# A causal convolution in 64x32 tiles, placed behind the second product slot

## The chip, the core and the metric

One core of a Trainium2 chip. The metric is the device time of one execution in microseconds (us); lower is better. Engines by the profile's names: PE (TensorE), PEld (its weight loads), DVE (VectorE), ACT (ScalarE), POOL (GpSimd), SP (SyncE, which issues most transfers).

## The reference

`x` is 8 x 4160 x 192 in float32. First a causal convolution along the sequence, 7 taps, one softmax-normalised set of taps for each of 8 heads of 24 channels; then, per token, a maximum of three linear maps and an output map:

```python
w = softmax(weight, axis=-1)                       # 8 heads x 7 taps
y[b, s, h, g] = sum_k w[h, k] * x_pad[b, s + k, h, g]   # x_pad: 6 zero rows ahead of the sequence
h = maximum(maximum(y @ w1, y @ w2), y @ w3)       # 192 -> 768
out = h @ w_out                                    # 768 -> 192, 33280 tokens, float32
```

## The kernel before

The 33,280 tokens are 65 blocks of 512. A block is 512 consecutive tokens of one sequence, or (one block) the last 64 tokens of all eight sequences. Every block goes through three steps:

- **conv**: `y`, turned so that channels lie on partitions, in float16, twice (each row half of the 128 partitions has all 192 channels in three 64-row pieces).
- **l1** (`L490`): six column tiles `j` of the hidden layer. w3 is subtracted from w1 and w2 beforehand (`wd`: upper rows w2 - w3, lower rows w1 - w3), so that a tile takes 3 matmuls on each half of the array's rows, 64 x 128, 512 columns. The lower half gives `lp`, the upper `lq`; ACT writes r = relu(lp) (`L503`), DVE writes h = max(r, lq) (`L504`).
- **st2** (`L508`): the output, 4 groups of 128 tokens, 30 matmuls of 192 columns on each half (`po`): `h` against `w_out`, and `y` against m = w3 w_out, which brings back what was subtracted. ACT copies one half's sum (`L560`), DVE adds the other (`L561`), SP stores.

The loop over block t (`L656`) is a software pipeline: l1 of block t and st2 of block t - 1 alternate, one column tile and 5 matmuls on each half at a time. I call such a pair a product slot; there are six in an iteration.

Conv is made in three ways. Blocks 0 to 3 by dense band matmuls (`conv_dense`, `L405`). The blocks of `qpos` (11, 16, ... 61 and 64; twelve) on POOL: load, cast, transpose by SP, then 7 taps (`tap_q`, `L221`: three products `L229` and a sum `L237` a tap), spread over the iterations by `plan`. All others on PE, block 4 alone and then in pairs: POOL casts the two x blocks to float16 (`cast_x`, `L165`), `conv` (`L387`) multiplies them by a band matrix, ACT and DVE copy the four results `G` out of PSUM to `ys` (`evac`), SP turns `ys` by a DMA transpose to `yd` (`turn`) and copies each half of `yd` across to the other (`double`).

In `conv` of before a tile has 64 tokens on 70 rows (64 and the 6 ahead), 16 matmuls with 192 columns, two places of 64 columns abreast:

```python
lhsT=band[0:HALF + PAD, h, PAD:HALF + PAD],
rhs=x16s[t0][0:HALF + PAD, h, c, :, :, :].rearrange("p u r c -> p (u r c)"),
start=True, stop=True, tile_position=(0, HALF * c))
```

It stands behind l1's first tile of the iteration, with one matmul of st2's lower half drawn ahead of it (`st2(t - 1, 0, NJ, True)`). The conv of a pair is made three iterations before its first block is used.

PSUM has 8 banks: `psp` and `psq`, two each, for lp and lq in turn; `psw`, four, for po. Conv takes two of psw and one each of psp and psq. Engines run their own instructions in the program's order; SP's order in an iteration is: load x of block t + 6, double block t + 2, a lane's transpose and lead-in rows, a lane's load, (after conv) turn block t + 3, store block t - 2.

Of the kernel before, what the change touches and what calls it, by code (L numbers as in the profile page):

```python
# [14 lines left out]
P = 128  # L15
# [12 lines left out]
def kernel(  # L28
# [42 lines left out]
    qpos = [q for q in range(11, NB - 3, EVERY)] + [NB - 1]  # L71
# [23 lines left out]
    NR = NBLK // HALF  # L95

    def rows_of(t):
        rows = [(b, S + o) for (b, S, N, off) in blocks[t] for o in range(0, N, HALF)]
        assert len(rows) == NR
        return rows  # L100
# [4 lines left out]
    xfp = ctx.enter_context(tc.tile_pool(name="xfp", bufs=6))  # L105
# [5 lines left out]
    ydp = ctx.enter_context(tc.tile_pool(name="ydp", bufs=6))  # L111
# [9 lines left out]
    xin = {}  # L121

    def load_x(t, eng=nc.sync):
        if not 0 <= t < NB or t in qset:
            return
        pool, tag = (xfp, "xf") if t > 1 else ((xap, "xa"), (xbp, "xb"))[t]
        xf = pool.tile([P, NR, D], FP32, tag=tag, name=f"xf_{t}")
        if t < NDENSE:
            todo = [(0, c[3], c[1] * SEQ + c[2]) for c in chunks_of[t]]
        else:  # L130
            todo = [(PAD, HALF, b * SEQ) if s == 0 else (0, HALF + PAD, b * SEQ + s - PAD)
                    for b, s in rows_of(t)]
        parts = []
        i, n = 0, len(todo)
        row = [c[2] for c in todo]
        while i < n:
            k = i
            while k + 1 < n and todo[k + 1][:2] == todo[i][:2] and row[k + 1] - row[k] == row[i + 1] - row[i]:
                k += 1
            step = row[i + 1] - row[i] if k > i else 0  # L140
            p0, rlen = todo[i][:2]
            src = bass.AP(tensor=x.tensor, offset=row[i] * D,
                          ap=[[D, rlen], [step * D, k - i + 1], [1, D]])
            eng.dma_start(out=xf[p0:p0 + rlen, i:k + 1, :], in_=src)
            if parts and parts[-1][0] == rlen:
                parts[-1] = (rlen, parts[-1][1], k + 1)
            else:
                parts.append((rlen, i, k + 1))
            i = k + 1
        xin[t] = [xf, todo[0][0], parts]  # L150
# [14 lines left out]
    def cast_x(t):  # L165
# [4 lines left out]
        if u == 0:  # L170
            x16s[t0] = x16p.tile([P, NHEAD, 2, nu, NR // 2, GRP], FP16, tag="x16", name=f"x16_{t0}")
        if p0:
            nc.gpsimd.memset(xf[0:p0, 0, :], 0.0)
        K = HALF + PAD
        for c in range(2):
            nc.gpsimd.tensor_copy(out=x16s[t0][0:K, :, c, u, :, :].rearrange("p h r c -> p r h c"),  # L176
                                  in_=xf[0:K, c:NR:2, :].rearrange("p r (h c) -> p r h c", c=GRP))


# [41 lines left out]
    def tap_q(q, k):  # L221
# [17 lines left out]
        yd = dense[q] = ydp.tile([P, 2, NCH // 2, P], FP16, tag="yd", name=f"yd_{q}")  # L239
# [41 lines left out]
    for t in range(2, 7):  # L281
        load_x(t)

# [3 lines left out]
    nc.gpsimd.tensor_copy(out=ident16[:], in_=ident[:])  # L287
    idle = const.tile([P, NBLK], FP16)
# [25 lines left out]
    for v in range(2):  # L314
        nc.gpsimd.memset(xz[1][v][:], 0.0)
    wcol16 = const.tile([P, 3, KW], FP16)
# [70 lines left out]
    def conv(t, pools):  # L387
# [4 lines left out]
        per = NHEAD // n  # L392
        w = nu * (NR // 2) * GRP
        G = [pool.tile([P, per, w], FP32, tag=tag, name=f"G{i}_{t}") for i, (pool, tag) in enumerate(pools)]
        for h in range(NHEAD):
            for c in range(2):
                nc.tensor.matmul(  # L397
                    G[h // per][HALF * c:HALF * (c + 1), h % per, :],
                    lhsT=band[0:HALF + PAD, h, PAD:HALF + PAD],
                    rhs=x16s[t0][0:HALF + PAD, h, c, :, :, :].rearrange("p u r c -> p (u r c)"),  # L400
                    start=True, stop=True, tile_position=(0, HALF * c))
        slots[t0] = ysp.tile([P, nu, NR // 2, D], FP16, tag="ys", name=f"ys_{t}")
# [35 lines left out]
    def evac(t, i, copy=nc.scalar.copy):  # L438
# [3 lines left out]
        per = NHEAD // len(G)  # L442
        copy(out=slots[t][:, :, :, GRP * per * i:GRP * per * (i + 1)].rearrange(  # L443
# [3 lines left out]
    def turn(t):  # L447


        if t >= NB or t in qset:  # L450
            return
        t0, u, nu = place(t)
        yd = dense[t] = ydp.tile([P, 2, NCH // 2, P], FP16, tag="yd", name=f"yd_{t}")
        nc.sync.dma_start_transpose(out=yd[:, 0, :, :],
                                    in_=slots[t0][:, u, :, :].rearrange("p r d -> p (r d)"))

    def double(t):

        if NDENSE <= t < NB:
            yd = dense[t]  # L460
            for i in range(2):
                nc.sync.dma_start(out=yd[HALF * i:HALF * (i + 1), 1, :, :],
                                  in_=yd[HALF * (1 - i):HALF * (2 - i), 0, :, :])

    def spot(t, i, c, r):
# [3 lines left out]
        else:  # L469
            own, k = (NC * r + c) % 2, (NC * r + c) // 2  # L470
        return k + (0 if own == i else NCH // 2)

    def y_all(t, i, c):
        row = slice(HALF * i, HALF * (i + 1))
        if t < NDENSE:
            return dense[t][row, c, :]
        a = dense[t][row, 0, 0, :]
# [5 lines left out]
    def y_tok(t, i, c, s):  # L483
        row = slice(HALF * i, HALF * (i + 1))
        if t < NDENSE:
            return dense[t][row, c, P * s:P * (s + 1)]
        k = spot(t, i, c, s)
        return dense[t][row, k // 6, k % 6, :]

    def l1(t, j, pools=((psp, "p"), (psq, "q"))):  # L490


        N = blkN[t]
        ps = [pool.tile([P, NBLK], FP32, tag=tag, name=f"l{tag}{i}_{t}_{j}")
              for i, (pool, tag) in enumerate(pools)]
        for c in range(NC):
            for i in range(2):
                row = slice(HALF * i, HALF * (i + 1))
                nc.tensor.matmul(ps[i][:, 0:N], lhsT=wd[row, c, P * j:P * (j + 1)],  # L499
                                 rhs=y_all(t, i, c),  # L500
                                 start=(c == 0), stop=(c == NC - 1))
        r = rp.tile([P, NBLK], FP16, tag="r", name=f"r_{t}_{j}")
        nc.scalar.activation(out=r[:, 0:N], in_=ps[0][:, 0:N], func=AF.Relu)  # L503
        nc.vector.tensor_max(out=hs[t][:, j, 0:N], in0=r[:, 0:N], in1=ps[1][:, 0:N])  # L504

    ahead = set()

    def st2(t, u, NU, first_half_only=False):  # L508
# [5 lines left out]
        hT = hs[t]  # L514
        if t not in halves:
            todo = [[], []]
            for s in range(4):
                for i in range(2):
                    row = slice(HALF * i, HALF * (i + 1))
                    mm = [(y_tok(t, i, i, s), m16[row, 0, :])]  # L520
                    if s % 2 == i:
                        mm.append((y_tok(t, i, 2, s), m16[row, 1, :]))
                    hh = [(hT[row, j, P * s:P * (s + 1)], wo[row, j, :]) for j in range(NJ)]
                    mm = hh + mm if t == 0 else mm + hh
                    todo[i] += [(s, n == 0, n == len(mm) - 1, m) for n, m in enumerate(mm)]
# [6 lines left out]
            halves[t] = (todo, {})  # L532
        todo, ps = halves[t]
        n = len(todo[0])
        es = range(n * u // NU, n * (u + 1) // NU)
        for e in es[:1] if first_half_only else es:
            for i in range(2):
                if first_half_only:
                    if i:
                        break  # L540
                    ahead.add((t, e))
                elif i == 0 and (t, e) in ahead:
                    continue
                s, first, last, (a, b) = todo[i][e]
                b0 = s if t == NB - 1 else s - s % 2
                if (b0, i) not in ps:
                    pool, tag = (psw, "w")
                    if t == NB - 1 and s in (1, 2):
                        pool, tag = (psp, "p") if i == 0 else (psq, "q")
                    ps[b0, i] = pool.tile([P, 2, D], FP32, tag=tag, name=f"po{i}_{t}_{s}")  # L550
                nc.tensor.matmul(ps[b0, i][:, s % 2, :], lhsT=a, rhs=b, start=first, stop=last)  # L551
            ends = {todo[i][e][0] for i in range(2) if todo[i][e][2]}
            for s in sorted(ends):
                done[t, s] = done.get((t, s), 0) + sum(todo[i][e][0] == s and todo[i][e][2] for i in range(2))
                if done[t, s] < 2 or (s % 2 == 0 and t < NB - 1):
                    continue
                s0 = s if t == NB - 1 else s - 1
                ss = slice(s0 % 2, s % 2 + 1)
                a = tp.tile([P, 2, D], FP32, tag="a", name=f"a_{t}_{s}")
                nc.scalar.copy(out=a[:, ss, :], in_=ps[s0, 0][:, ss, :])  # L560
                nc.vector.tensor_add(out=outs[t][:, s0:s + 1, :], in0=a[:, ss, :],  # L561
                                     in1=ps[s0, 1][:, ss, :])
                if t == NB - 1 and s == 1:
                    store(t, 0, 2, (nc.sync,))
                elif t == NB - 1 and s == 3:
                    store(t, 2, 3, (nc.scalar,))
                    store(t, 3, 4, (nc.sync,))
# [17 lines left out]
    def begin(t):  # L585
        hs[t] = hp.tile([P, NJ, NBLK], FP16, tag="h", name=f"h_{t}")
# [168 lines left out]
```

## Time and profile before

| | |
|---|---|
| median of 3 runs | 464.19 us (463.25 to 464.36) |
| the profiled execution | 464.5 us, span 462.7 us, clock granted 1.0 throughout |
| PE po, line 551 | 3120 + 780 matmuls of 192 columns, 243 ns each |
| PE lp and lq, line 499 | 2 x 1158 matmuls recorded, 512 columns, 376 ns each |
| PE G, line 397 | 400 matmuls, 248 ns each; 400 weight loads |
| POOL taps, lines 229, 237, 240 | 252 x 478 ns, 60 x 1809 ns, 12 x 1814 ns |
| POOL casts, line 176 | 98 x 822 ns |
| copies of G, line 443 | ACT 49 x 484 ns, DVE 49 x 550 ns |
| transfers | 80.77 MB, mean 175 GB/s; queue 1 busy 79.1% of 16 engines' span |

The matmul durations overlap: a matmul's row runs from its start to its end at the far side, while the next one on the same rows starts earlier. Distances between starts say what a matmul occupies. The span begins with the first instruction and ends with the last; some 1.8 us of the execution lie around it.

### The profile page before, as it was taken

To read this page: it belongs to the slowest core of one execution; us is meant where nothing else is said; L and a number is where in the kernel's file an instruction comes from. 1 tells how busy PE (TensorE), PEld (TensorE's weight loads), DVE (VectorE), ACT (ScalarE), POOL (GpSimd) and SP (SyncE) were. 2 spreads that over 40 slices of the span, in tenths; PEclk is the share of its full clock that TensorE was granted. 3 is DMA by queue.
4 is the path that set the end of the run, shared out by engine and by line. 5 is a ranking of instruction groups with operands and counts; after the bars stand their busy time and mean duration, and the time that the engine had idled before them with its cause. 6 is when DMAs were issued, how large, how long until landed. Compare 5 with 4: busy or idle time off the path is not lost.

```text
span 462.7 us, 17259 instructions
## 1 busy us (share of the span) xinstructions
PE 454.4 (98%) x6969; PEld 367.9 (80%) x6969; DVE 354.1 (77%) x595; ACT 314.3 (68%) x597; POOL 352.6 (76%) x501
## 2 busy tenths in 40 slices
PE   8999999999999999999999999999999999999997
PEld 4576788977877887888888888888888888888886
DVE  6777777777778787777878777777777777777775
ACT  5766566667676666767667676676767676676664
POOL 5753289999988978978967978978957969979500
PEclk9999999999999999999999999999999999999999
DMA  8959999999869878787789697698598797884423
GB/s 190 222 127 198 177 209 179 192 209 224 192 130 231 170 155 211 175 181 183 166 175 198 157 211 165 157 213 198 132 210 179 164 224 176 144 191 92 100 70 103
DMA packets 137527, 80.77 MB, mean 175 GB/s; under 512 B 58294, under 2 KB 137368, under 8 KB 137448
## 3 DMA queue, kind: packets, MB, share of 16 engines
q1 hardware_dynamic: 137176, 79.18, 79.1%
q8 instruction: 54, 0.88, 0.9%
q0 software_dynamic: 112, 0.39, 0.3%
q14 instruction: 25, 0.20, 0.2%
q10 hardware_dynamic: 160, 0.10, 0.1%
HBM read 29.85 MB, written 25.56 MB: 120 GB/s over the span
## 4 chain that ended last, share of the span: by engine, by line
PE 89%; POOL 5%; DMA 4%; issue 1%; DVE 0%; ACT 0%; POOLq 0%; DVEq 0%; SPq 0%
PE lq L499 35%; PE po L551 33%; PE lp L499 14%; PE G L397 4%; POOL tap L237 2%; POOL tap L229 2%; DMA yd<-ys 1%; PE idle L294 1%; DMA xt<-xq 1%; DMA yd<-yd 1%; PE D L415 1%; POOL x L176 1%; DMA xt<-xt 1%; PE lw L499 0%; PE band_cols L335 0%
## 5 line engine op out<-in xcount | busy, mean ns | idle before, releaser
L504 DVE TENSOR_TENSOR h<-r,lq 128x512 f16<-128x512 f16 x386 | 264.7, 686 | 99.5 <-ACT r L503 99.4
L503 ACT ACTIVATE r<-lp 128x512 f16<-128x512 f32 x386 | 230.5, 597 | 134.7 <-PE lp L499 123.8
L499 PE MATMUL lp<-yd,wd 64*128 64x512 f16 x1158 | 312.3, 376 | 2.2 <-DMA yd<-yd 1.6
L499 PE MATMUL lq<-yd,wd 64*128 64x512 f16 x1158 | 312.3, 376 | 0.3 <-DVE yd L431 0.3
L551 PE MATMUL po<-wo,h 64*128 64x192 f16 x3120 | 263.8, 243 | 0.7 <-issue 0.7
L551 PEld LDWEIGHTS <-h 64*128 64x128 f16 x3120 | 209.2, 94 | 22.2 <-issue 0.9
L499 PEld LDWEIGHTS <-wd 64*128 64x128 f16 x2340 | 160.9, 94 | 39.4 <-DMA yd<-yd 2.1
L176 POOL CAST x<-xf 70x768 f16<-70x768 f32 x98 | 77.8, 822 | 60.6 <-DMA xf<-in_x_dram 54.0
L229 POOL TENSOR_SCALAR tap<-xt,wcol 128x256 f32<-128x256 f16 x252 | 116.1, 478 | 3.9 <-DMA xt<-xt 3.3
L237 POOL TENSOR_TENSOR tap<-tap,tap 128x768 f32<-128x768 f32 x60 | 108.6, 1809 | 5.0
L551 PE MATMUL po<-m,yd 64*128 64x192 f16 x780 | 109.4, 243 | 0.0
L561 DVE TENSOR_TENSOR o<-a,po 128x384 f32<-128x384 f32 (+1 forms) x132 | 71.4, 541 | 1.2 <-ACT a L560 1.2
L551 PEld LDWEIGHTS <-yd 64*128 64x128 f16 x780 | 61.9, 94 | 11.8
L560 ACT COPY a<-po 128x384 f32<-128x384 f32 (+1 forms) x132 | 62.3, 473 | 3.0 <-PE po L551 3.0
L443 DVE CAST ys<-G 128x384 f16<-128x384 f32 x49 | 24.9, 550 | 0.6 <-PE G L397 0.6
L397 PEld LDWEIGHTS <-band 70*64 70x64 f16 x400 | 15.8, 109 | 9.9 <-PE lp L499 9.0
L240 POOL TENSOR_TENSOR yd<-tap,tap 128x768 f16<-128x768 f32 x12 | 21.8, 1814 | 1.0
L397 PE MATMUL G<-x,band 70*64 70x192 f16 (+1 forms) x400 | 21.2, 248 | 0.7 <-POOL x L176 0.5
L443 ACT CAST ys<-G 128x384 f16<-128x384 f32 x49 | 21.0, 484 | 0.8 <-PE G L397 0.8
L198 POOL CAST xq<-xl 128x384 f16<-128x384 f32 x24 | 11.4, 505 | 0.0
L256 POOL CAST xz<-xf 112x80 f16<-112x80 f32 (+2 forms) x18 | 5.2, 330 | 4.5 <-DMA xf<-in_x_dram 4.5
L294 PE MATMUL idle<-idle 128*128 128x512 f16 x15 | 6.4, 573 | 1.2 <-DVE idle L289 1.2
(52 smaller groups left out, 68.6 us busy)
## 6 DMA issues: line engine op xcount, KB each, us to landing
out_dram<-o SPq DMA_DIRECT2D x61, 384.0 KB
xf<-in_x_dram SPq DMA_DIRECT2D x47, 420.0 KB
yd<-yd SPq DMA_DIRECT2D x122, 96.0 KB
xl<-in_x_dram SPq DMA_DIRECT2D x12, 384.0 KB
xf<-in_x_dram SPq DMA_DIRECT2D x5, 367.5 KB
ws<-in_moe_w_dram SPq DMA_DIRECT2D x6, 192.0 KB
out_dram<-o SPq DMA_DIRECT2D x5, 192.0 KB
yd<-ys SPq DMA_TRANSPOSE x49
```

Of the source, the lines that this page charges most:

```text
L176: nc.gpsimd.tensor_copy(out=x16s[t0][0:K, :, c, u, :, :].rearrange("p h r c -> p r h c"), in_=xf[0:K, c:NR:2, :].rearrange("p r (h c) -> p ...
L229: nc.gpsimd.tensor_scalar(out=part[:, 2 * c:2 * c + 2, :], in0=xt[:, 2 * c:2 * c + 2, LEAD - PAD + k:LEAD - PAD + k + P], scalar1=wcol[:, ...
L237: nc.gpsimd.tensor_add(out=accs[q][:], in0=accs[q][:], in1=part[:])
L240: nc.gpsimd.tensor_add(out=yd[:, 0, :, :], in0=accs.pop(q)[:], in1=part[:])
L397: nc.tensor.matmul(G[h // per][HALF * c:HALF * (c + 1), h % per, :], lhsT=band[0:HALF + PAD, h, PAD:HALF + PAD], rhs=x16s[t0][0:HALF + PAD ...
L443: copy(out=slots[t][:, :, :, GRP * per * i:GRP * per * (i + 1)].rearrange("p u r (h c) -> p h (u r) c", c=GRP), in_=G[i][:].rearrange("p h ...
L499: nc.tensor.matmul(ps[i][:, 0:N], lhsT=wd[row, c, P * j:P * (j + 1)], rhs=y_all(t, i, c), start=(c == 0), stop=(c == NC - 1))
L503: nc.scalar.activation(out=r[:, 0:N], in_=ps[0][:, 0:N], func=AF.Relu)
L504: nc.vector.tensor_max(out=hs[t][:, j, 0:N], in0=r[:, 0:N], in1=ps[1][:, 0:N])
L551: nc.tensor.matmul(ps[b0, i][:, s % 2, :], lhsT=a, rhs=b, start=first, stop=last)
L560: nc.scalar.copy(out=a[:, ss, :], in_=ps[s0, 0][:, ss, :])
L561: nc.vector.tensor_add(out=outs[t][:, s0:s + 1, :], in0=a[:, ss, :], in1=ps[s0, 1][:, ss, :])
```

## The change

- **Conv's tiles**: 32 tokens on 39 rows (32 and 7 ahead), in both row halves and in four column places, so eight places; 64 matmuls for a pair, 96 columns each. An x block is loaded as 16 pieces of 39 rows, 8 below and 8 above, in two DMAs instead of one; the rows between are zeroed once by POOL (six buffers, now constant tiles). A cast covers 103 partitions; its free size stays 768.
- **Its place**: behind l1's second column tile of the iteration. Ahead of it stand 7 of st2's lower matmuls and 3 of its upper ones (`OWN`, `AHEAD`), the upper half's four follow after it. The slots behind it are filled by `ROOM`: st2 is at 5, 13, 17, 21, 26, 30 matmuls at the end of the slots instead of 5, 10, 15, 20, 25, 30.
- **The order of matmuls**: the halves have queues of their own (`lanes`); `emit` writes out the one with fewer columns so far, `meet` empties both ahead of conv. Before, they alternated strictly. What ACT, DVE and SP do after certain matmuls (`op`) is written out when these have been.
- **Turn and double**: both transposes of a pair directly behind conv; one doubling of both blocks (two DMAs of 192 KB instead of four of 96) two iterations ahead of the first of them, on SP now in front of the x load.
- **Ten GpSimd blocks** (15, 20, ... 60) instead of twelve: 25 pairs on PE instead of 24. The first taps are in iteration 8 instead of 5, over five iterations.
- **The store of block 0** moves from POOL to SP; stores of block t - 2 are still in iteration t, now ahead of turn.

The core of the diff:

```diff
-    qpos = [q for q in range(11, NB - 3, EVERY)] + [NB - 1]
+    qpos = [q for q in range(15, NB - 4, EVERY)]
...
+    TOK = 32
+    NR = NBLK // TOK // 2
+    LAP = PAD + 1
+    KR = TOK + LAP
...
         for h in range(NHEAD):
-            for c in range(2):
-                nc.tensor.matmul(
-                    G[h // per][HALF * c:HALF * (c + 1), h % per, :],
...
+            for j in range(4):
+                for i in range(2):
+                    row = slice(HALF * i, HALF * i + KR)
+                    nc.tensor.matmul(
+                        G[2 * (h // per) + i][TOK * j:TOK * (j + 1), h % per, :],
+                        lhsT=band[row, h, HALF * i + LAP:HALF * i + KR],
+                        rhs=x16s[t0][row, h, j, :, :, :].rearrange("p u r c -> p (u r c)"),
+                        start=True, stop=True, tile_position=(HALF * i, TOK * j))
...
+    def emit(rest=False):
+        run_ops()
+        while lanes[0] or lanes[1]:
+            i = 0 if clock[0] <= clock[1] else 1
+            if not lanes[i]:
+                if not rest:
+                    return
+                i = 1 - i
+            cols, fn = lanes[i].popleft()
+            fn()
+            clock[i] += cols
+            gone[i] += 1
+            run_ops()
+
+    def meet():
+        emit(True)
+        assert not ops
+        clock[0] = clock[1] = 0
...
+        st2(t - 1, (cuts[0], cuts[0]))
         for j in range(1, NJ):
             l1(t, j)
-            st2(t - 1, j, NJ)
+            if late and j == 1:
+                st2(t - 1, (cuts[0] + OWN + AHEAD, cuts[0] + OWN))
+                meet()
+                conv(u, WPWQ)
+                for i in (0, 2):
+                    evac(u, i)
+                for i in (1, 3):
+                    evac(u, i, nc.vector.tensor_copy)
+                turn(u)
+            st2(t - 1, (cuts[j], cuts[j]))
```

## The prediction

> **What bounds the kernel now.** I read the page's busy shares first, then the chain that ended last, then single stretches of TensorE (PE) in the timeline, then the waits.
>
> ```profile
> PE 454.4 (98%) x6969; PEld 367.9 (80%) x6969; DVE 354.1 (77%) x595; ACT 314.3 (68%) x597; POOL 352.6 (76%) x501
> PE 89%; POOL 5%; DMA 4%; issue 1%; DVE 0%; ACT 0%; POOLq 0%; DVEq 0%; SPq 0%
> ```
>
> PE is the bound. But a busy PE is not a full one: the question is what it streams in each stretch. The chain, in order of time, gives the beat (two convolutions, shown with what follows them):
>
> ```profile
> 114.57 0.85 PE G L397 x16
> 115.42 0.52 PE po L551 x9
> 116.59 0.40 PE po L551 x8
> 117.65 0.40 PE po L551 x8
> ...
> 128.25 0.85 PE G L397 x16
> ```
>
> One product slot (an `l1` of 3+3 matmuls of 512 columns, then 5+5 of 192 columns, lower and upper row half abreast) takes 1.06 us (116.59 to 117.65), six slots a block, 6.36. The convs of pairs start at 114.57, 128.25 and, 5 blocks after the first, at 148.33: 33.76 us for 30 slots (31.80) and two convs. So one pair's conv costs (33.76 - 31.80) / 2 = 0.98 us of PE. Where that goes is seen in the timeline of PE:
>
> ```profile
> 114.07 0.38 PE L499 MATMUL lp<-yd,wd 64*128 64x512 f16 x1
> 114.27 0.38 PE L499 MATMUL lq<-yd,wd 64*128 64x512 f16 x1
> 114.28 0.24 PE L551 MATMUL po<-m,yd 64*128 64x192 f16 x1
> 114.57 0.27 PE L397 MATMUL G<-x,band 70*64 70x192 f16 x2
> ...
> 115.35 0.26 PE L551 MATMUL po<-m,yd 64*128 64x192 f16 x2
> ```
>
> A 512-column matmul holds its half 0.216 us (lp to lp in these rows), a 192-column one 0.082. The lower half is free at 114.36, the upper (it runs 0.2 late) at 114.48; G begins at 114.57, 0.09 after the later half; its 16 matmuls stream until 115.25; the products begin again 0.10 later. So 0.98 = 0.11 lower half idle + 0.09 + 0.68 + 0.10.
>
> **The conv, part by part.** Before: 24 pairs and one single block, 16 matmuls each, two abreast. After: 25 pairs and a single, 64 matmuls of 96 columns on 39 rows and 32 columns, eight places. Rows that bound one such conv:
>
> ```profile
> 28.33:28.80 0.47, 0.47 (x40) 0.47 (x42) 1.00 0.00 0
> 29.35:29.70 0.35, 0.34 (x16) 0.35 (x16) 1.00 0.00 0
> ```
>
> These are two stretches of PE, the first of the dense conv (line 415, four 32-column places abreast, 103 columns), the second of the single block's conv (line 397, two abreast, 96 columns). The second says that a 96-column round takes 0.35 / 8 = 0.043 us; the first that four places abreast still keep this rate (10 rounds in 0.47, 0.047 for 103 columns). That two row halves run abreast, every slot shows. Eight abreast no row shows. Lower bound: 64 / 8 = 8 rounds, 0.34 us. Upper bound: PE takes in no more than the first row's 40 matmuls and 42 loads in 0.47, so 64 pairs in 0.74; 16 rounds, if the halves do not overlap here, give 0.69. I take 0.37, near the lower end, because the first row scaled with the columns and not with the count.
>
> The Trainium skill (TensorE: Matmul & The Clock Gate, Part 3, "Measured speedup vs the span model") puts a further place at some 4 ns; by that 64 would need an estimated 0.26 us and streaming would bind; by the dense row's rate it would be 0.74 and nearly all of the gain gone. No run here shows eight places.
>
> Around it: the 0.09 and 0.10 stay (the tile form still changes twice). The 0.11 goes if both halves end together: the lower half takes 7 second products, the upper 3, and the upper's four go after the conv, so each half has the same work from conv to conv. But conv results must leave PSUM before the next slots. With the rows' durations (relu 0.597, max 0.686, ys copies 0.484 on ACT and 0.550 on DVE), from the moment E when the halves end: DVE finishes the max of slot 1 at E+0.95, its two copies at E+1.4 and E+1.9; slot 2's upper product wants that max at E+0.96, slot 3's products want the two buffers at E+1.6 and E+2.0; the second pair of po tiles wants ACT's two copies (E+1.0, E+1.5) at E+1.45 and E+1.8. All fit within 0.05. So one conv: 0.09 + 0.37 + 0.10 + 0.04 = 0.60 (bounds 0.55 and 0.93, or 0.25 more if DVE comes late).
>
> Sum: 25 x 0.60 = 15.0 instead of 24 x 0.98 = 23.5: **-8.5 us**. The single block's conv, 0.35 now, lies between 0.17 (8 rounds of 48 columns) and 0.74; it is put at no change, since the transfer after it ends later anyway.
>
> **GpSimd.** Two conv blocks fewer take 2 x (21 x 0.478 + 5 x 1.809 + 1.814 + 2 x 0.505 + 0.19) = 44 us off POOL; four more casts (0.822, free size unchanged) and six zero fills (1,536 columns; from the 960 of line 315 in 0.892, 1.4 each) add 12. POOL is off the path but for one place:
>
> ```profile
> 80.08 0.24 PE L397 MATMUL G<-x,band 70*64 70x192 f16 x1
> 80.84 0.82 PE L397 MATMUL G<-x,band 70*64 70x192 f16 x15 [0.53 <-POOL x L176]
> ```
>
> Here the first lane's taps, packed into three iterations, keep the cast late; with what precedes it PE loses 1.0. The first lane now starts its taps at iteration 8 instead of 5 and spreads them over five: **-1.0**. The fills lie in the start, where POOL waits 4.5 us for loads.
>
> **SyncE and transfers.** A pair's two transposes now go together, a slot and a half later, and the next iteration's doubling waits for them, with the x loads behind it on SP (before, the load went first). Issue to landing, by the semaphores: transposes 2.8, doubles 4.7, x loads 6.1 us (medians after 100 us). From an iteration's start: copies done 4.1, second transpose landed 4.1 + 1.25 + 2.8 = 8.2, that is 1.2 into the next (6.96 long); doubles issued by 2.4, landed about 7.5, wanted at 13: covered by 5 us. Loads issued by 3.0, landed 9.1, cast 1.6, wanted by the conv in the iteration after at 15.3 on the same count: spare 4.4. Cover gone, each us late costs each conv a us. The stores moved to SP are issues of 0.5 us of outputs finished an iteration ago: nothing behind them waits. In the start PE waits twice for doubles:
>
> ```profile
> PE lp L499 <- DMA yd<-yd: 1.6, 2, 0.9
> ```
>
> With the drain before them they are 1.1 us (block 4) and 0.9 (block 5). Block 4 gets a second transpose (1.3 us of issue) in its way; block 5's doubling loses the load and store that stood in front of it. They may vanish (-1.9) or grow by 1: put at 0. At the end the upper half trails by two 192-column matmuls more: +0.15.
>
> An x block grows from 8 x 70 to 16 x 39 rows, 420 to 468 KB. A five-block beat moves 33.76 us x 182 GB/s (200 to 300 us) = 6.14 MB now and 6.34 in 33.0 us after, 192 GB/s; 40 to 80 us already moved 198, and the share there was 1.01 against 0.82. So it fits, with less air.
>
> The Trainium skill speaks against this edit (DMA: Bandwidth & Descriptors, "Why a DMA increments its semaphore by 16 and not by 1"): the engines used are the largest number up to 16 that divides the outer row counts, 14 for 70 rows, 13 for 39. By it the x share would sit on 13 engines, 36 KB of a block on each instead of 30, and my estimate of a beat on those (1.92 MB / 13 + 4.42 MB / 16, at 198 GB/s / 16) is 34 us instead of 33.0: no gain left, some 464. The shares of this trace are means over 16 engines and cannot show it.
>
> **Sum.** -8.5 - 1.0 + 0 + 0.15 = -9.3. Span 462.7 becomes 453.4; the profiled execution took 464.5, 1.8 around its span: 455.2; the median of the runs, 464.19, lies 0.3 lower: **455.0 us**.
>
> **Rivals.** (a) PE's intake, or halves that do not overlap: conv 0.69 to 0.74, 25 x 0.92 = 23.0, so -0.5 - 1.0: 462.7. For it: no row shows more than about 87 matmuls a us; against: that row was set by its columns. (b) DVE comes late behind the conv, 0.25 us each: 25 x 0.25 = 6.2, 461. For it: the margins above are under 0.1 us; against: POOL and ACT leave DVE's 77% as it is. (c) Slower: x loads land late because they queue behind the doubling and are larger. Place: conv waits for POOL's cast. It decides once a landing takes over 6.1 + 4.4 = 10.5 us; the start shows 11.7 with five loads queued; with 11.0 each conv waits 0.5: +12.5, 467.5. Against: the longest after 100 us is 7.6.
>
> **Chances.** Forecast 0.66 (452 to 458), (a) 0.17, (b) 0.08, (c) 0.09. The measurement tells about 0.3%, 1.4 us, from no change; (a) straddles that, half faster, half the same. Faster 0.82, same 0.09, slower 0.09. The range takes the forecast with both waits of the start gone and the lower bound of conv (451.5), and (b) with most of (a): up to 462.
>
> **What would show it.** Right: convs of pairs 13.3 us apart where they are 13.68 now, G's 64 matmuls within 0.4 us, no POOL wait before G, slots still 1.06. Wrong: G rows of 0.7 us (a); lp or lq rows with idle before them ended by DVE (b); G waiting for POOL's x, and POOL for xf, in every pair (c).

## The result, and the profile after

The changed kernel takes **483.42 us** (median of 4 runs, 478.41 to 486.16); the kernel before, beside it on the same chip, 463.82. The profiled execution is the longest of the four, 486.16 us, span 484.4; it lies over 1.5% above the shortest, counts as slow and is left out of the ratio, which is 1.0387 over the other three, interval 1.0307 to 1.0467: slower by 4%, where 2% faster was forecast. In the changed kernel `conv` is line 419, the copies of G 466, `turn` 480, `double` 493, the x load 166, the cast 198, l1 570 to 578, st2 627.

The profile's page first, busy shares and the chain that ended last:

```profile
PE 458.3 (95%) x8233; PEld 421.3 (87%) x8233; DVE 361.2 (75%) x597; ACT 314.9 (65%) x599; POOL 320.2 (66%) x450
PE 65%; DMA 23%; SPq 3%; POOL 3%; DVE 3%; issue 2%; ACT 1%; POOLq 0%; DVEq 0%
```

Before, PE held 89% of the chain and transfers 4%. Now a quarter of the span hangs on transfers. The chain in order of time shows one stretch of it (start, duration, what):

```profile
207.96 6.20 DMA yp<-ys
214.21 0.47 SPq L493
214.72 0.60 SPq L493
215.37 0.56 SPq L166
215.97 5.90 DMA xf<-in_x_dram
...
222.77 0.84 POOL x L198
223.65 0.78 PE G L419 x64
```

The transposes of a pair (`yp<-ys`) take 6.2 us; SyncE's doubling (`SPq L493`) waits for them, and the x load (`L166`), queued behind the doubling, is issued only then; it lands 5.9 us later, POOL casts, and the conv that wanted this x can start. That conv is late, so is its turn, and so the next load. Medians from issue to landing after 100 us: transposes 6.0 us (2.8 before), stores 5.3 (3.3), x loads 5.2 (6.1, in DMAs of 420 KB instead of 234). The waits say the same (total, times, longest; the first row is the kernel before, where the third was not among the larger ones):

```profile
POOL x L176 <- DMA xf<-in_x_dram: 54.0, 26, 4.3
```

```profile
POOL x L198 <- DMA xf<-in_x_dram: 110.1, 29, 11.1
...
PE G L419 <- POOL x L198: 12.4, 8, 2.4
```

Two other things show. First, the conv itself, undisturbed, in the timeline of PE:

```profile
154.45 0.24 PE L627 MATMUL po<-m,yp 64*128 64x192 f16 x1
154.63 0.75 PE L419 MATMUL G<-x,band 39*32 39x96 f16 x64
155.31 0.25 PE L627 MATMUL po<-wo,h 64*128 64x192 f16 x1
```

Undisturbed convs follow each other after 13.506 and 19.866 us, 33.37 for 30 slots of 1.06: (33.37 - 31.80) / 2 = **0.787 us** a conv, not 0.60. Second, the start: block 2's first `h` comes 3.9 us later than before. Set block against block with the kernel before, 3.9 us are lost by block 2, and the other losses stand at single places (blocks 9, 11, 14, 28 to 29, 34, 39, 54, 59; 0.4 to 4.0 us each, 18.6 together); in between an undisturbed conv gains 0.2 us. Of the 18.6, 12.4 are the eight waits of a conv for a cast (the row above); 1.5 are a wait of l1 at block 11 for an `h` that DVE made late, because a store was late to free its buffer; and three stretches at half clock (last section) come to an estimated 5.1. Together that is 19.0.

### The profile page after: what moved, and what is told of

Read it like the earlier page. It is cut to its first block, busy times and chain, and to the rows that moved or that the text cites. A ratio compares the mean times of both kernels' runs of the same rounds, so it can differ in the third digit from the quotient of the medians.

```text
span 484.4 us, 19750 instructions
## 1 busy us (share of the span) xinstructions
PE 458.3 (95%) x8233; PEld 421.3 (87%) x8233; DVE 361.2 (75%) x597; ACT 314.9 (65%) x599; POOL 320.2 (66%) x450
## 4 chain that ended last, share of the span: by engine, by line
PE 65%; DMA 23%; SPq 3%; POOL 3%; DVE 3%; issue 2%; ACT 1%; POOLq 0%; DVEq 0%
PE po L627 23%; PE lq L570 21%; PE lp L570 15%; DMA yp<-ys 11%; DMA xf<-in_x_dram 10%; PE G L419 3%; POOL x L198 2%; SPq L493 2%; DMA yp<-yp 2%; SPq L166 1%; DVE yd L453 1%; PE D L437 1%; DVE xz L276 1%; POOL tap L249 1%; PE lw L570 1%
## 5 line engine op out<-in xcount | busy, mean ns | idle before, releaser
L627 PE MATMUL po<-wo,h 64*128 64x192 f16 x3120 | 338.7, 244 | 0.0
L627 PEld LDWEIGHTS <-h 64*128 64x128 f16 x3120 | 248.2, 95 | 6.0
L570 PE MATMUL lp<-yp,wd 64*128 64x512 f16 x918 | 251.7, 381 | 1.7 <-DMA yp<-yp 1.6
L570 PE MATMUL lq<-yp,wd 64*128 64x512 f16 x918 | 250.3, 380 | 2.3 <-DVE h L578 1.5
L198 POOL CAST x<-xf 103x768 f16<-103x768 f32 x102 | 81.3, 826 | 112.1 <-DMA xf<-in_x_dram 110.1
L627 PE MATMUL po<-m,yp 64*128 64x192 f16 x612 | 120.9, 245 | 0.0
L627 PEld LDWEIGHTS <-yp 64*128 64x128 f16 x612 | 56.8, 95 | 0.7
L570 PE MATMUL lp<-yq,wd 64*128 64x512 f16 x180 | 48.5, 376 | 0.0
L570 PE MATMUL lq<-yq,wd 64*128 64x512 f16 x180 | 48.5, 377 | 0.0
L466 ACT CAST ys<-G 128x384 f16<-128x384 f32 x51 | 22.1, 481 | 23.6 <-PE G L419 21.4
L419 PE MATMUL G<-x,band 39*32 39x96 f16 (+1 forms) x1664 | 19.6, 208 | 13.2 <-POOL x L198 12.4
L570 PE MATMUL lq<-yd,wd 64*128 64x512 f16 x60 | 17.4, 389 | 1.8 <-DVE yd L453 1.6
```

The lines of the kernel that those rows point to most:

```text
L198: nc.gpsimd.tensor_copy(out=x16s[t0][0:K, :, :, u, r, :].rearrange("p h j c -> p j h c"), in_=xf[0:K, 4 * r:4 * r + 4, :].rearrange("p j ( ...
L419: nc.tensor.matmul(G[2 * (h // per) + i][TOK * j:TOK * (j + 1), h % per, :], lhsT=band[row, h, HALF * i + LAP:HALF * i + KR], rhs=x16s[t0] ...
L466: copy(out=slots[t][:, i % 2, :, :, GRP * h0:GRP * (h0 + per)].rearrange("p u r (h c) -> p h (u r) c", c=GRP), in_=G[i][:].rearrange("p h ...
L570: nc.tensor.matmul(ps[i][:], lhsT=wd[HALF * i:HALF * (i + 1), c, P * j:P * (j + 1)], rhs=y_all(t, i, c), start=(c == 0), stop=(c == NC - 1))
```

## The experiments

Two theories stood first. *Order*: the load stands behind a doubling that waits for late transposes. *Volume*: the x traffic of 39-row pieces loads the transfers, whatever the order.

**Load first.** SyncE's order of before, in the changed kernel:

```diff
+        if t > 3:
+            load_x(t + 6)
         for v in doubles_at.get(t, ...):
             double(v)
-        if t > 3:
-            load_x(t + 6)
```

> The changed kernel with one edit: the x load of block t + 6 is issued ahead of the doubling of block t + 2, as in the kernel before. Order theory (the load stands behind a doubling that waits for a late transpose, and the chain transpose, doubling, load, cast, conv sets the beat): GpSimd's wait for x falls from 110 us to under 50, convs of pairs come back to 13.5 and 19.9 us apart, and the time is 462 to 467 us. Volume theory (16 pieces of 39 rows load all transfers more, whatever their order): conv still waits for the cast in most five-block beats, transposes still take about 6 us from issue to landing, and the time stays above 475.

467.53 us (464.6 to 471.35), ratio 1.0074 (1.0031 to 1.0116): 15.9 us come back. Its profiled execution is its shortest, 464.6. After the start every pair of convs is 13.506 or 19.866 us apart, and PE has no wait for a cast left. SyncE's timeline and POOL's wait in this kernel:

```profile
194.13 2.55 SPq L480 DMA_TRANSPOSE yp<-ys  x2
196.72 1.03 SPq L166 DMA_DIRECT2D xf<-in_x_dram  x2
198.31 1.11 SPq L493 DMA_DIRECT2D yp<-yp  x2
```

```profile
POOL x L198 <- DMA xf<-in_x_dram: 59.3, 22, 7.2
```

The load goes out straight behind the transposes' issue and the doubling waits behind it; the transposes themselves are faster again (3.5 us median). In the changed kernel the held loads and stores had gone out together, straight ahead of the next turn. The late transpose was partly made by the chain it belongs to, it seems; no run tries the crowding alone.

**The order alone, in the kernel before.** The same swap the other way round:

```diff
-        if t > 4:
-            load_x(t + 6)
         for u in doubles_at.get(t, (t + 2,)):
             double(u)
-        if t == 4:
+        if t > 3:
             load_x(t + 6)
```

> The kernel before with one edit: the x load of block t + 6 is issued behind the doubling of block t + 2, as in the changed kernel. Order theory: if the order alone is enough, 3 us or more are lost, 467 to 480. If it needs the pair of transposes sent together, later in the iteration, as well (one transpose of 2.8 us lands in time here), no change, 463 to 465, and GpSimd's wait for x stays at 54 us.

463.98 us, ratio 1.0007 (0.9977 to 1.0038): nothing. The order does act, though: the transposes' median goes from 2.8 to 4.8 us and SyncE's waits for them from 40 to 113 us in total, but no conv waits; this kernel has the room. So the order needs a partner. Two more runs put the rest of the changed kernel's order into the kernel before, first the pairs turned and doubled together, then also the later place:

```diff
-            turn(t + 3)
+            turn(u)          # if a conv stands in this iteration
+            turn(u + 1)
```

> The kernel before with SyncE's order as in the changed one: the x load behind the doubling, both transposes of a pair directly behind its conv, and both blocks doubled together two iterations ahead of the first (two buffers more for the turned blocks). Tiles, place, bytes of x and GpSimd's blocks stay those of before. Queue theory (the order on SyncE is enough, once the doubling waits for a pair sent together): conv waits for casts, GpSimd's wait for x rises from 62 us to 80 and more, 468 to 480. Sum theory (the load is late only when the order meets the later place and the 11% more bytes of x, 16 pieces of 39 rows): no conv waits for a cast, 463 to 466.

465.83 us, 1.0024 (0.9992 to 1.0056).

```diff
             l1(t, j)
+            if j == 1 and t > 2 and u < NB:
+                st2(t - 1, 1, NJ, True)
+                conv(u, WPWQ)
+                ...
+                turn(u)
+                turn(u + 1)
             st2(t - 1, j, NJ)
```

> The kernel before with all of the changed kernel's order on SyncE (load behind the doubling, store ahead of the turn, pair turned and doubled together) and, beyond that, conv behind the second column tile. Tiles, bytes of x and GpSimd's twelve blocks stay those of before. Place theory (order and late turn together make the chain, 1.5 us later than in the run before this one): conv waits for casts, 470 and more. Bytes theory (the chain closes only with the changed kernel's x traffic): 464 to 468.

466.22 us, 1.0052 (1.0026 to 1.0078), and in its trace from block 11 to 64 each block follows the one before it as in the kernel before, to 0.01 us; where the 0.5% lies is not shown, as the profiled execution (464.15) is one of the shorter ones. Order and place, complete, cost the tiles of before nothing in the steady part. The place theory falls.

**An earlier place in the changed kernel.**

```diff
+        if late:
+            st2(t - 1, (AHEAD, 0))
+            meet()
+            conv(u, WPWQ)
+            ...
+            turn(u)
         st2(t - 1, (cuts[0], cuts[0]))
```

> The changed kernel with conv, copies and turn one place earlier: behind the first column tile, with four lower second products ahead of it (as in the kernel before), instead of behind the second; the x load still stands behind the doubling. Order theory, second half (the load's wait needs the late transposes): the turn is issued some 1.5 us earlier in the iteration, its pair lands before the doubling or little after it, GpSimd's wait for x falls from 110 us to under 70, and the time to 463 to 472. If the order alone sets the beat, the stalls stay, 476 and more.

485.01 us (477.85 to 487.45), 1.0369: no better. In its profiled execution (its shortest, 477.9) the larger stalls behind the start stand at blocks 9 to 14 and 59, and SyncE still waits 77.8 us for the transposes (80.0 in the changed kernel); so an earlier turn doesn't open the chain. The second half of the theory, that an earlier turn would be enough, was wrong.

**The doubling an iteration later**, the load still behind it:

```diff
-            [v for v in (t + 2,) if ...]
+            [v for v in (t + 1, t + 2) if (v == t + 2 if v in qset else v == t + 1 and ...)]
```

> The changed kernel with a pair's doubling issued one iteration later (for block t + 1 instead of t + 2, from the pair 7, 8 on); the x load still stands behind it. Order theory, made sharper: it is SyncE's wait for the late transposes, at the head of the iteration, that holds the load back; here the transposes are a whole iteration old when the doubling is issued, so nothing is held: GpSimd's wait for x under 60 us, no conv that waits for a cast after block 14, 463 to 469. If what matters is only that loads and transposes bunch together in an iteration: stalls stay, 475 and more. New danger: the doubling must land within an iteration (6.4 us; 3 to 6 from issue), and l1 may wait for it.

472.74 us (468.75 to 477.08), 1.0148 (1.0099 to 1.0197): 10.7 us of 483.4 come back with the load still behind the doubling, because the doubling hardly waits any more (SyncE's waits for transposes: 8.2 us in total, 80.0 in the changed kernel). From block 11 to 64 there are two stalls, 1.0 and 1.2 us, and neither is a wait for x (they are of the kind told at the end). The rest, 9 us by block 10, is lost in the start, l1 of block 7 waiting for its doubles (3.0 us) among it: the new danger, which I had put too low.

**The x traffic.** More rows to a tile:

```diff
-    LAP = PAD + 1
+    LAP = PAD + 2        # 40 rows; PAD + 10 for 48
```

> The changed kernel with 40 rows to a tile instead of 39 (8 ahead instead of 7); 2.6% more bytes of x, the same work otherwise. Order theory: within 5 us of the changed kernel's 478 to 486. Share theory (the rows decide how many engines carry an x load): by the Trainium skill's page DMA: Bandwidth & Descriptors, section Why a DMA increments its semaphore by 16 and not by 1, 40 rows use 10 engines and 39 use 13; then the x loads take visibly longer (from 5.2 us median to 6 or more) and the time passes 490.

490.15 us (487.39 to 494.36): 6.7 more. x loads 5.0 us at the median, not slower. The changed kernel's own runs lie 8 us apart, so this doesn't tell 2.6% more bytes from fewer engines.

> The changed kernel with 48 rows to a tile (16 ahead instead of 7): 23% more bytes of x. Share theory: 48 rows go on all 16 engines, x loads get no slower and the time falls below 475. Volume theory: 2.9 MB of x a beat instead of 2.3 at 180 GB/s are 3 us more a beat of 33 us, 495 us and more. Order theory: somewhat longer landings in the same chain, 483 to 492.

509.72 us (506.77 to 512.03): 26 more; the volume theory, not the share theory, at this size. The same with the load first:

> Load-first kernel with 48 rows to a tile: 23% more bytes of x, which cost the changed kernel 26 us. If bytes cost time only through the chain that the order closes: 467 to 472. If they cost time by themselves (transfers at their limit): 485 and more.

488.88 us, 21.4 more than load first with 39 rows: bytes cost time by themselves. PE's waits are then for doubles (16.6 us), no longer for casts. The windows from 100 to 400 us of this kernel, of the changed one, of the one before and of the best kernel below (39 rows, load first) (us, PE, PEld, DVE, ACT, POOL busy; clock, DMA share, GB/s):

```profile
100.00:400.00 300.00, 288.80 (x5120) 266.47 (x5116) 224.92 (x374) 198.98 (x375) 238.19 (x328) 0.99 1.06 192
```

```profile
100.00:400.00 300.00, 290.74 (x5218) 276.25 (x5214) 226.33 (x379) 200.27 (x378) 239.61 (x332) 0.99 0.95 181
```

```profile
100.00:400.00 300.00, 300.00 (x4553) 245.49 (x4550) 233.27 (x392) 207.95 (x392) 252.36 (x350) 1.00 0.83 184
```

```profile
100.00:400.00 300.00, 300.00 (x5467) 286.88 (x5465) 236.08 (x396) 209.45 (x396) 252.20 (x348) 1.00 0.94 192
```

The forecast's beat needed 192 GB/s (6.34 MB in 33.0 us). The best kernel moves that at share 0.94 and load first 189 at 0.90, and no conv waits in either: the bytes of 39 rows fit. With 48 rows and work always waiting (share 1.06) no more than 192 came. 5.6 MB more at 192 GB/s are 29 us; 21 were lost, so by this estimate load first had about 8 us to spare over its whole run. Half of x, the other way (the upper eight of an x block's 16 pieces are never loaded, so half of its x is missing):

```diff
-                     ... for i, (b, s) in enumerate(rows_of(t))]
+                     ... for i, (b, s) in enumerate(rows_of(t)[:NR])]
```

> The changed kernel without the second DMA of each x load from block 4 on (the upper eight of 16 pieces are left out: 234 KB a block instead of 468, and half the pieces; each buffer is zeroed whole). Order and place are those of the changed kernel. Bytes theory: the chain opens, transposes land in 3 to 4 us instead of 6, no conv waits for a cast after block 14, 462 to 468. Place theory: the doubling still waits for the late pair and the load for the doubling; 472 and more.

463.54 us, 0.9995 (0.998 to 1.001). Its window:

```profile
100.00:400.00 300.00, 300.00 (x5469) 286.81 (x5466) 236.23 (x396) 209.57 (x397) 252.12 (x349) 1.00 0.73 160
```

Order and place are the changed kernel's, the load waits for the doubling as there, and no conv waits: transposes land in 3.0 us. So the chain is closed by both together: the order puts the load behind the transposes, and with the x traffic on top the transposes are too late. Take away either and it opens. Half of x also halves the x loads that SyncE issues; bytes and issues were not told apart.

**Rows and engines.** In the best kernel (below), 38 rows:

```diff
-    LAP = PAD + 1
+    LAP = PAD
```

> The kernel with the load first and the start put right (462.7 us) with 38 rows to a tile, 6 ahead instead of 7: 2.6% fewer bytes of x, the least that the taps allow. If rows decide how many engines carry a load (the Trainium skill, DMA: Bandwidth & Descriptors, Why a DMA increments its semaphore by 16 and not by 1: 38 rows go on 2 engines), each 228 KB of a DMA on two of 16 engines take an estimated 20 us at 5.6 GB/s an engine (90 over 16, half of 180 GB/s) to 10 at 11; landings of 10 us and more, every conv waits, over 490. If rows do not matter: 461 to 464.

**802.24 us**, for 2.6% fewer bytes of x. The window, and a wait:

```profile
100.00:400.00 300.00, 192.74 (x3040) 174.40 (x3040) 133.92 (x220) 116.78 (x220) 124.17 (x174) 0.81 0.56 105
```

```profile
POOL x L198 <- DMA xf<-in_x_dram: 366.8, 44, 21.8
```

Loads land after 10.7 us at the median (5.6 with 39 rows) while the transfers stand half idle (share 0.56). The rule cited in the prediction, that the row count decides the engines, holds here. The traces show it in the steps by which a landing load counts up its semaphore: an x load in full rows has 14 late steps in the kernel before (70 rows), 13 with 39 rows, 10 with 40, 16 with 48 and 2 with 38, as many as the rule gives engines; SyncE's other transfers in the loop have 16. The price at 38 rows is far above what I expected. By the rule 39 rows go on 13 engines and 70 on 14; how much of the changed kernel's loss comes from that one engine and how much from 11% more bytes was not told apart.

**The conv.** Each matmul cut in two, in load first:

```diff
+                    for v in range(nu):
-                        ... rhs=x16s[t0][row, h, j, :, :, :]      # 96 columns
+                            ... rhs=x16s[t0][row, h, j, v, :, :]  # 48 columns
```

> Load-first kernel (467.5 us) with each conv matmul of 96 columns cut into two of 48: 128 weight loads and matmuls, the same columns, the same result. Columns theory (what streams is the columns, as the forecast had it): no change, 465 to 469. Intake theory (past some 32 pairs taken ahead, PE takes in a weight load and a matmul in 8.35 ns, as the second half of a conv shows in the changed kernel's trace): 64 more pairs at 8.35 ns are 0.53 us for each of 25 convs, 13 us more, 478 to 483, and a conv's second stretch still runs at 8.35 ns a pair. By the Trainium skill's page TensorE: Matmul & The Clock Gate, Part 3, Measured speedup vs the span model, some 4 ns a place: an estimated 0.26 us a conv, 474.

507.73 us, 40 more than load first, three times what the intake theory expected. Between undisturbed blocks a conv costs 0.54 us more: 64 pairs (a weight load and a matmul) at 8.4 ns, as this expectation had it; the 4 ns a place that it cites would be half of it. 25 times that is 13.5. Most of the rest are stalls of a kind of their own, shown in the last section. In load first the 64 matmuls start so: 31 intervals in 0.163 us, a gap of 0.08, 31 intervals in 0.31 (10 ns each).

> Load-first kernel with a pair's conv in two parts of 32 matmuls, heads 0 to 3 behind the second column tile and heads 4 to 7 behind the third; the turn follows the second part, one slot later. Intake theory: each part runs within the pairs taken ahead, 0.09 + 0.16 + 0.10, so 0.70 us for a conv instead of 0.787: undisturbed convs 13.42 and 19.78 us apart instead of 13.505 and 19.867, and no stretch at 8.35 ns a pair. If the slower second half is due to something else (PSUM, the second set of banks): 0.79 + 0.19, 13.7 apart. The time depends on whether the turn is now too late: 465 to 480.

481.25 us, 1.0363. The matmuls of both parts of 32 start within 0.163 us, as the intake theory says and the other doesn't: the slow second half is neither PSUM nor the second banks. But a conv costs 0.57 us more, not 0.09 less, by waits that I had not counted:

```profile
PEld L575 <- issue: 16.4, 32, 0.8
...
PE po L632 <- ACT ys L471: 8.3, 24, 0.3
```

The second product's bank (`po`) now waits for ACT's copy of the first part.

**The start.** GpSimd's fills in the kernel before, into an unused tile:

```diff
+    def fill():
+        nc.gpsimd.memset(spare[32:64, :, :], 0.0)
+    fill()
+    fill()
...
         nc.gpsimd.memset(xz[1][v][:], 0.0)
+    fill()
```

> The kernel before with GpSimd's six zero fills of 32 x 1536 added at the places where the changed kernel has them, into a tile that nobody reads. Start theory (the fills slow VectorE's copies and casts of the start, which run 4.16 and 3.33 us instead of 2.87 and 1.77 in the changed kernel's profile, and set the start back by 3.9 us): 465 to 468. Cover theory (they lie where GpSimd waits anyway, as the prediction had it): 462.5 to 464.5.

468.07 us, 1.0069 (1.0041 to 1.0097): 3.2 us by the ratio, for work that nobody reads. The timelines of POOL and DVE with the fills (in the longest run, 471.6), then DVE before:

```profile
7.53 1.37 POOL L290 MEMSET spare<- 32x1536 f32 x1
```

```profile
4.79 4.17 DVE L256 CAST xz<-xf 112x240 f16<-112x240 f32 x3 [1.63 <-DMA xf<-in_x_dram]
```

```profile
4.32 2.87 DVE L256 CAST xz<-xf 112x240 f16<-112x240 f32 x3 [1.18 <-DMA xf<-in_x_dram]
```

The three casts take 1.30 us more, about the one fill of 1.37 beside them. It is the third cast, 1.47 us instead of 0.18. The kernels with half of x and with the later doubling show the same (4.19); in load first the fill falls just behind the casts, and they take 2.89. The Trainium skill (SBUF — State Buffer, "Who interferes with whom") names a mechanism: DVE in its two-port mode and GpSimd share a pair of ports, and who comes second waits for the whole instruction. The durations agree; whether these casts ran in that mode no run here shows.

Two kernels change the start on top of load first. The first moved blocks 9 and 10's loads behind the doubling of block 5:

```diff
-    load_x(6)                              # amid VectorE's copies
     make_wd(4, 6, nc.gpsimd)
+    load_x(6)
+    load_x(7)
...
+        if t == 4:
+            load_x(9)
+            load_x(10)
```

> Load-first kernel with the start put right: the fills of blocks 6 and 7 behind the weights' last subtraction instead of amid VectorE's copies, block 7's load with the first loads, ahead of block 4's transposes, and the loads of blocks 9 and 10 behind the doubling of block 5. Start theory: the waits for doubles at blocks 4 and 5 (7.6 us in the load-first profile) fall below 5, DVE's casts take under 3 us, and the time is 461 to 465. If the start is set by something else: 466 to 469.

467.7 us, no gain: blocks 5 and 6 come 1.3 us early, then block 7 loses 3.9: its transposes are issued behind those four loads and block 7's l1 waits for them. The second loads 7, 8 and 9 early instead:

```diff
     make_wd(4, 6, nc.gpsimd)
+    load_x(6)
+    load_x(7)
...
     cast_dense(2, ...)
-    get_x(7)
+    load_x(8)
...
     cast_x(4)
+    load_x(9)
```

> Load-first kernel with the start put right in another way: the fills of blocks 6 and 7 behind the weights' last subtraction, those of 8 and 9 behind the casts of blocks 2 and 3, and the loads of blocks 7, 8 and 9 as soon as their buffers are free, ahead of block 4's transposes, into the stretch from 24 to 32 us in which the transfers stand idle. Start theory: blocks 2 to 9 are no later than in the kernel before, the rest gains 0.19 us a conv, 459 to 463. If the doubles of blocks 5 and 7 are late again: 465 to 468.

**462.72 us** (460.51 to 464.75), ratio to the kernel before 0.9974 (0.9952 to 0.9997): the only complete version below the kernel before, by a quarter of a per cent. It is its shortest run that was profiled, 460.51:

```profile
PE 451.0 (98%) x8233; PEld 418.6 (91%) x8233; DVE 355.5 (78%) x597; ACT 314.7 (69%) x599; POOL 320.6 (70%) x450
```

## Why the prediction was wrong, step by step

- **"Spare 4.4 us" and "covered by 5 us" failed**: this step lost the forecast. It wrote down the right queue (load behind doubling behind transposes) and priced it with medians of the old trace, transposes of 2.8 us at share 0.83. In the changed kernel transposes take 6.0 us and stores 5.3 (3.3); the doubling waits for them, the load behind it goes out too late, and convs wait 12.4 us for their casts, with the half clock after some of these waits on top. Price: 483.4 - 467.5 = 15.9 us. Neither part does it alone: with the load first the transposes take 3.5 us, with half of x 3.0, and with the order alone, in the kernel before, 4.8 without a loss.
- **"So it fits, with less air" was right on the bytes**: load first moves 189 GB/s at share 0.90 without a stall, the best kernel 192 at 0.94. What it left out is that latencies grow while the bytes still fit.
- **Rival (c) had the right path, at a chance of 0.09.** Its deciding point was wrong: not a landing over 10.5 us (the median was 5.2, the longest 8.8), but a late issue.
- **The term 0.37 was mis-sized.** The conv's matmuls start within 0.55 us, and the conv costs 0.787 instead of 0.60: 25 x 0.187 = 4.7 us. "That row was set by its columns" held for 32 matmuls; of rival (a), PE's intake was the right part, with too high a price (0.92). (The bounds 0.55 and 0.93 come out as 0.57 and 0.97 by the step's own four terms; 0.787 lies within either.)
- **The fills, which got no term, cost time**: 3.2 us in the kernel before. I asked whether POOL was idle there, not whom it slows.
- **The start's two waits, put at 0**: moving the early loads and with them the fills was worth 467.5 - 462.7 = 4.8 us.
- **Right**: slots stay at 1.06; the first lane's stall goes (in the best kernel block 10 gains 0.9 beyond the conv's share); from the last block's first `h` to the end the best kernel takes 0.18 us longer (0.15 forecast); DVE does not come late behind a conv (no PE wait for `h` over 0.2 us in load first and the best kernel). That the 44 us off GpSimd move nothing was not tried alone.
- **The rule on engines** (14 to 13) gave an estimated beat of 34 us; load first shows 33.37 with no stall, so it didn't bind at 39 rows. At 38, on the same kernel but for one row, it cost 339 us.

The sum: 455.0 + 4.7 (conv) = 459.7 against the best kernel's 462.7 (its profiled execution 460.5); 462.7 + 4.8 (start) = 467.5 and 467.5 + 15.9 (chain) = 483.4 are differences of measured kernels. The 3.0 us between 459.7 and 462.7 are not assigned; that kernel's runs lie 4.2 us apart.

## What to carry to other kernels

When a change adds bytes to transfers that are over 0.8 busy, as here, the latencies of the old trace are no longer prices: that the bytes fit says nothing of who waits behind whom. In a queue, keep an early transfer ahead of one whose own condition can be late; with this x traffic that order was worth 3%, with that of before nothing. An idle engine is not free if the work put on it slows a neighbour.

## What the hardware did that I had not expected

**PE's instructions come in blocks.** In the kernel with 128 matmuls a conv, PE stops with nothing to wait for:

```profile
266.55 0.38 PE L571 MATMUL lq<-yp,wd 64*128 64x512 f16 x1
270.17 0.58 PE L571 MATMUL lp<-yp,wd 64*128 64x512 f16 x1 [3.25 <-issue]
```

From 80 us to the program's end it has ten such stops over 0.7 us, 17.0 us in all. Counting the recorded instructions of PE and its queue from 0 in order of time, every one of the ten ends at a number 193 above a multiple of 256. The profile's page lists transfers that fit:

```profile
q8 instruction: 77, 1.26, 1.1%
```

77 packets, 16.4 KB each, for 19,666 recorded instructions of PE: 255 a packet (258 in the kernel before), each packet 0.9 to 1.8 us in transfer after 80 us. Each of the ten stops ends 1.2 to 1.7 us after such a packet has landed. A conv of 256 instructions that start within 1.1 us uses up a packet's worth. With 128, one stop of 1.0 us stands at such a place in the changed kernel, and the two late stalls of the kernel that doubles later do. Why the packets come late was not tried. The four stretches at half clock that follow such stops last 17 us in all, an estimated 8.5 lost; with the 17.0 of the stops and the conv's 13.5 that is 39 of the 40 us.

**The clock falls after a stop.** Windows of the changed kernel around a conv that waits for x (the clock is the third number from the end):

```profile
117.00:119.50 2.50, 0.32 (x8) 0.18 (x5) 0.72 (x2) 0.37 (x1) 1.38 (x2) 1.00 0.76 236
119.50:124.00 4.50, 4.24 (x96) 3.72 (x97) 2.17 (x4) 1.97 (x5) 3.93 (x6) 0.62 1.08 205
```

A stop of 2.4 us is followed by a stretch at half clock, 3.4 us within the second window, which costs an estimated 1.7 us more, half of it. After the start this happened three times. In the 3.4 us ahead of each PE stood idle for 2.4, 2.2 and 1.7 us; three other waits, of 1.6 to 1.9 us, were not followed by it, and there the idle time in any 3.4 us stretch (counted in steps from the drops) stayed under 1.6. The kernel before kept 1.00 throughout.
